# PSUM tiles of one bank in the attention and channel stages, made over into pairs for the last phase

## The chip, the cores and the metric

The kernel runs on one core of a Trainium2 chip. PE (TensorE) multiplies into PSUM, a memory of eight banks of 512 float32 columns on 128 partitions; DVE (VectorE) and ACT (ScalarE) read results out of it; POOL (GpSimd) works on data in SBUF; SP issues the DMAs. The metric is the time of one execution on the device, in microseconds (us), as a median over runs.

## What is computed

Attention under a mask of blocks, then a mixer over tokens and channels, then an RWKV layer. The weights of the mixer and of the last layer are 64-bit floating-point words; the kernel splits each into a high and a low float32 part on the chip, and what they multiply too, so that a product takes three matmuls.

```python
# B, H, S, D = 4, 8, 576, 64; a position sees the blocks of 64 up to its own
attn = softmax(mask(q @ k.T / 8)); x = (attn @ v) as [B, S, 512]
h = relu(x.T @ w_tok1) @ w_tok2              # tokens: 576 -> 256 -> 576
u = x + h.T
u = u + relu(u @ w_ch1) @ w_ch2              # channels: 512 -> 1536 -> 512
xp = u moved on by one token
k = relu((mu_k * u + (1 - mu_k) * xp) @ w_k) # 512 -> 1024
r = sigmoid((mu_r * u + (1 - mu_r) * xp) @ w_r)
out = r * (k * k @ w_v)
```

## The kernel before, in words

Attention works on 16 pairs of heads. For a pair, PE multiplies q by k into PSUM (`emit_s`), DVE takes each row's maximum while it applies the mask and writes the shifted scores to SBUF (`emit_max`, L376), ACT takes the exponential (L381), POOL scales by the reciprocal of the sum (L390), PE transposes the result into PSUM (`emit_t`, L399 and L401), ACT or DVE copies it to SBUF (tiles pt), and PE multiplies by v, both heads and several blocks accumulating in one bank (`emit_pv`), copied into the tile u of the batch. For every two pairs the token mixing of their columns comes in between the work on later pairs: PE transposes u (L655), ACT and DVE split the transposed data into a high and a low part (xnh, xnl, the latter by L673), PE multiplies (k1), ACT and DVE split again (h1h L700, h1l L704), PE multiplies (k2), and DVE adds the result to u (ku, L729).

The channel stage (L, O) goes over five slabs of 460 or 464 tokens: for each of twelve blocks of 128 hidden channels a product into a bank of the lower half, split by ACT (L966) and DVE (L969), then four products that accumulate over the blocks in four banks of the upper half; at a slab's end DVE adds these to u (L996). The last phase goes over the four batches with products K, V and R, seven block products each, whose results stand in two banks side by side and are read by one instruction over both (`wide`; L1122 and L1126, for instance). Weights come page by page: a DMA, some integer work on ACT, DVE and POOL, and a split by POOL or ACT and by L218.

The order of all work is set beforehand. The class `Plan` holds every operation with its cost, priority and buffers, and plays them on a clock of its own; an operation is recorded on its engine when the planned time of all that it needs has come. PSUM is the ring `one` of eight slots, each a bank. A slot is given out when all users of the one before are done in the planned time; among free ones the longest free is taken. `lo4` and `hi4` take of the lower and the upper half, `two` takes two adjacent slots. Slots 6 and 7 are held for the score blocks of full width, 576 columns, until attention's last maximum.

Planned times only fix the order on each engine. What an engine waits for when the kernel runs is put in afterwards by the framework, from the instructions' reads and writes of tiles. In the kernel before PSUM consists of four tiles of two banks (L274), and a slot is half of one:

```python
banks = [ps1.tile([128, 2, 512], F32, name=f"bank{k}") for k in range(4)]
def bank(key):
    i = plan.slot["one", key]
    return banks[i // 2][:, i % 2]
def wide(key):
    return banks[plan.slot["one", key] // 2][:, :, 0:T]
```

Of the kernel before, what the change touches and what calls it, by code (L numbers as in the profile page):

```python
# [8 lines left out]
F32 = mybir.dt.float32  # L9
# [8 lines left out]
PSUM = bass.MemoryType.PSUM  # L18
# [4 lines left out]
T = 288  # L23
# [43 lines left out]
class Plan:  # L67
# [40 lines left out]
    def slots(self, n, done):  # L108

        want, got, at = {}, [], 0.0  # L110
        for tag, _ in self.ops[n][4]:
            want[tag] = want.get(tag, 0) + 1
        for tag, k in want.items():
            can = []
            ring, part = self.PART.get(tag, (tag, None))
            for i in range(len(self.taken[ring])) if part is None else part:
                keys = {x for x in self.taken[ring][i:i + 1 + (tag == "two")] if x}
                users = [u for key in keys for u in self.users[key]]
                if all(u in done for u in users):
                    can.append((max([done[u] + self.LAT for u in users], default=0.0), i))  # L120
            if len(can) < k:
                return None, tag
            can.sort()
            got += [(tag, i) for _, i in can[:k]]
            at = max(at, can[k - 1][0])
        return at, got
# [10 lines left out]
    def run(self):  # L137
        ops = self.ops
        waiting = {n: len(set(o[1])) for n, o in ops.items()}
        after = {n: [] for n in ops}  # L140
        for n, o in ops.items():
            for d in set(o[1]):
                after[d].append(n)
        ready = {n for n, w in waiting.items() if not w}
        done, free, where, now = {}, {}, {}, "f"
        self.taken = {t: [None] * n for t, n in self.rings.items()}
        for tag, i, key in self.held:
            self.taken[tag][i] = key
        self.order = []
        while len(done) < len(ops):  # L150
            best, starts = None, {}
            for n in ready:
                room = 0.0
                if ops[n][4]:
                    room, _ = self.slots(n, done)
                    if room is None:
                        continue
                can = []
                for e, c in ops[n][0].items():
                    at = max(room, free.get("turn", 0.0) if self.turns(n, e) else 0.0)  # L160
                    r = max([at] + [done[d] + (0.0 if where[d] == e else ops[d][5]) for d in ops[n][1]])
                    pri = ops[n][3]
                    if e == "PE":
                        c += self.SWITCH * (self.mode[n] != now)
                        pri -= 0.25 * (self.mode[n] == now)
                    can.append((max(r, free.get(e, 0.0)), pri, n, c, e))
                end = min(x[0] + x[3] for x in can)
                for x in can:
                    if x[0] + x[3] <= end + 0.2:
                        starts.setdefault(x[4], []).append(x[:4])  # L170
            for e, cand in starts.items():
                first = min(c[0] for c in cand)
                t, p, n, c = min((c for c in cand if c[0] <= first + 0.02), key=lambda c: (c[1], c[0], str(c[2])))
                if best is None or (t, p, str(n), t + c, e) < best[:5]:
                    best = (t, p, str(n), t + c, e, n, c)
            if best is None:
                raise RuntimeError("stuck: " + "\n".join(f"{n} {self.slots(n, done)[1]}" for n in ready))
            t, _, _, _, e, n, c = best
            if ops[n][4]:
                got = self.slots(n, done)[1]  # L180
                for (tag, i), (_, key) in zip(sorted(got), sorted(ops[n][4], key=lambda a: a[0])):
                    ring = self.PART.get(tag, (tag,))[0]
                    self.taken[ring][i] = key
                    self.slot[ring, key] = i
                    if tag == "two":
                        self.taken[ring][i + 1] = key
            if e == "PE":
                now = self.mode[n]
            free[e] = t + c
            if self.turns(n, e):  # L190
                free["turn"] = t + c
            done[n], where[n] = t + c, e
            ready.remove(n)
            for m in after[n]:
                waiting[m] -= 1
                if not waiting[m]:
                    ready.add(m)
            self.order.append((t, e, n))
            self.record(ops[n][2], e)
# [3 lines left out]
def attn_mixer_rwkv_kernel(ctx: ExitStack, tc: tile.TileContext, z, v, vl, wt1, wt2, wc1, wc2, wk, wv, wr, mu, out):  # L203
    nc = tc.nc
    PE, ACT, DVE, POOL, SP = nc.tensor, nc.scalar, nc.vector, nc.gpsimd, nc.sync
    plan = Plan(tc)
# [13 lines left out]
    def mm(o, l, r, start, stop, more=False):  # L220
        PE.matmul(o, lhsT=l, rhs=r, start=start, stop=stop, skip_group_check=more)  # L221
# [48 lines left out]
    vs = [att2.tile([128, 4, 128], F32, name=f"vs{s}") for s in range(3)]  # L270
    vd = [att2.tile([128, 5, 128], F32, name=f"vd{s}") for s in range(3)]
    att3 = tc.alloc_tile_pool(name="att3", bufs=1, side="right")
    ps1 = tc.alloc_tile_pool(name="ps1", bufs=1, space=PSUM)
    banks = [ps1.tile([128, 2, 512], F32, name=f"bank{k}") for k in range(4)]  # L274
    pools = {}
    tl = {}


    def bank(key):

        i = plan.slot["one", key]
        return banks[i // 2][:, i % 2]

    def wide(key):

        return banks[plan.slot["one", key] // 2][:, :, 0:T]

    def warm(k):
        t = bank(("warm", 0))
# [48 lines left out]
    def s_part(p, h, i, cut):  # L338

        t, zt, hs = tl["s", p, h, i], tl["z", p], slice(64 * h, 64 * h + 64)  # L340
        q = zt[hs, S - 64 + 128 * i:S + 64 + 128 * i]
        k0 = (S - KE[i]) * h
        return [(t[:, COL[i] + a:COL[i] + e], q, zt[hs, k0 + a:k0 + e], True, True) for a, e in zip(cut, cut[1:])]

    def emit_s(p, step):
        if step < 2:
            a, b = (0, 1) if step == 0 else (1, 0)
            tl["s", p, a, 4] = banks[3].rearrange("p a b -> p (a b)")
            tl["s", p, b, 3] = tl["s", p, b, 0] = bank(("c", p, b, 3))
            x = s_part(p, a, 4, (0, 288, 576))  # L350
            y = s_part(p, b, 3, (0, 224, 448)) + s_part(p, b, 0, (0, 64))
        else:
            x, y = [], []
            for h, w in ((0, x), (1, y)):
                tl["s", p, h, 2] = tl["s", p, h, 1] = bank(("c", p, h, 2))
                w += s_part(p, h, 2, (0, 320)) + s_part(p, h, 1, (0, 192))
        for k in range(max(len(x), len(y))):
            for w in (x, y):
                if k < len(w):
                    mm(*w[k])  # L360
# [22 lines left out]
    def emit_rec(p, h, a, e):  # L383
        st = tl["st", p, h]
        DVE.tensor_tensor(st[:, 2, a:e], st[:, 1, a:e], eps[:, a:e], ALU.add)  # L385
        DVE.reciprocal(st[:, 2, a:e], st[:, 2, a:e])
# [55 lines left out]
    for p in range(NP):  # L442
        w = p - 3
# [9 lines left out]
        for h in range(2):  # L453
            for i in range(5):
                step = 2 if i in (1, 2) else (h if i == 4 else 1 - h)
                key = ("c", p, h, {0: 3, 1: 2}.get(i, i))
                f = p - 1.9 + 0.1 * step + 0.03 * {4: 0, 3: 1, 0: 2, 2: 0, 1: 1}[i] + 0.01 * h
# [5 lines left out]
                    lambda e, p=p, h=h, i=i: emit_max(p, h, i), f,  # L463
# [5 lines left out]
            for g, (a, b) in enumerate(((0, 3), (3, 5))):  # L469
                add(("rc", p, h, g), "DVE", 0.36, [("e", p, h, i) for i in range(a, b)],  # L470
                    lambda e, p=p, h=h, a=a, b=b: emit_rec(p, h, a, b), p - 2.5, uses=[("st", p, h)])
        for g, (diag, off) in enumerate(GROUPS):
# [3 lines left out]
                lambda e, p=p, g=g: emit_t(p, g), p - 1.0 + 0.07 * g,  # L476
# [163 lines left out]
    for b in range(B):  # L640
        for g in range(2):
# [33 lines left out]
            for c2 in range(3):  # L675
                n = 512 if c2 < 2 else 256
                key = ("xt", b, g, c2)
# [3 lines left out]
                    lambda e, f=xh, c2=c2: f(e, c2=c2), pb - 3, alloc=[] if c2 else [("xn", xk)], uses=[key] + ([xk] if c2 else []))  # L681
# [24 lines left out]
            for m in range(2):  # L706
                key, hk = ("k1", b, g, m), ("h1", b, g, m)
# [23 lines left out]
            for c in range(2):  # L731
                for p in range(2):
                    key = ("k2", b, g, p, c)
                    add(key, "PE", 6 * c_mm(T), [(s, b, g, m) for s in ("h1h", "h1l") for m in range(2)]
                        + [(s, "t2", 2 * c + k) for s in ("hi", "lo") for k in range(2)],
                        lambda e, f=k2, p=p, c=c: f(e, p=p, c=c), pb + 0.2 + 0.01 * c, alloc=[("dense", key)],
                        uses=[("h1", b, g, 0), ("h1", b, g, 1)], lat=0.3)
                    add(("ku", b, g, p, c), "DVE", c_dve(T), [key] + [("xt", b, g, k) for k in range(3)],
                        lambda e, f=ku, p=p, c=c: f(e, p=p, c=c), pb - 3, uses=[key])
# [21 lines left out]
    for nm, f in pages:  # L761
        tag = ("w" if f < 8 else "wx") if nm == "c1" else "w2a" if f < 4 else "w2b"
# [11 lines left out]
        n, k = PAIR.get((nm, f), (0, 0))  # L774
# [34 lines left out]
    for i in range(B):  # L809
        for n in range(7):  # L810
            for q in range(2):
                name = ("ld", "k", i, q, n)
                fetch_op(name, last + made_in("k", q, n, 0), ("W", "k", i, q, n), ("k", q, n, 0), "w", None if i == 0 else 130.0 + 16 * i - 9 + 0.1 * n)
                last = [name]
        for n in range(7):
            name = ("ld", "r", i, n)
# [116 lines left out]
    for t in range(NX):  # L933
        w = XS[t]
# [21 lines left out]
        for f in range(12):  # L956
            key, hk = ("lb", t, f), ("h", t, f)
# [26 lines left out]
        for f in range(12):  # L984
            for ms in ([(m,) for m in range(4)] if f in (0, 11) else [(0, 1, 2, 3)]):
# [3 lines left out]
                    lambda e, f=f, O=O, ms=ms: O(e, f=f, ms=ms), p0 + 1.2 + 0.5 * f + 0.01 * ms[0],  # L989
# [49 lines left out]
    for i in range(B):  # L1039
        b = order[i]  # L1040
# [233 lines left out]

    plan.run()
    pools["w2b"].release()
    ps1.release()
    pools["xp"].release()
    wp.release()
    glob.release()  # L1280
# [51 lines left out]
```

## Time and profile before

| what | us |
|---|---|
| median of 3 runs | 796.91 (794.59 to 796.92) |
| the profiled execution in all | 796.9 |
| its span, first to last instruction | 795.1 |
| PE busy | 761.4 |
| PE weight loads busy | 698.9 |
| DVE, ACT, POOL busy | 535.1, 399.5, 275.6 |

A stage's rate is set by the engine that is never idle in it; the idle time of the others costs nothing. So the table says little by itself, and the windows by stage and the list of waits say where PE stands and for whom. A matmul's end is modelled, and matmuls overlap: records of 0.28 us may follow each other every 0.12 us. In the rows, L221 is the helper that records most matmuls, so that the names of the tiles tell them apart: `bank<-z` are scores, `bank<-pt,vs` and `bank<-pt,vd` the products with v, `bank<-xnh,w1h` the first product of the token mixing, `bank<-w2h,h1h` the second, `bank<-xhl,w` and `bank<-hpB,w` those of the channel stage and the last phase. L211 and L213 are the helpers that copy on ACT and DVE.

### The profile page before, as it was taken

Reading aid. Unit: us, or ns where it says so; the run is one execution under the profiler, and the core shown is the slowest. Engines: PE = TensorE matmul, PEld = TensorE weight load, DVE = VectorE, ACT = ScalarE, POOL = GpSimd, SP = SyncE. Lnnn points to the kernel's source line nnn. Section 1 sums busy time; section 2 is a strip of 40 time slices with the busy share of each in tenths; the row PEclk is TensorE's granted clock in tenths of the full one; section 3 lists DMA queues with packets and bytes.
Section 4 is the critical chain, followed back from the end, with each engine's and each line's share of the span. In section 5 each row is a group of like instructions: output and inputs, shape, how many; then the busy total and the mean of one; then the engine's idle time right before and its main releaser. Section 6 shows DMA issues by size and latency. Waiting matters only on the chain.

```text
span 795.1 us, 14514 instructions
## 1 busy us (share of the span) xinstructions
PE 761.4 (96%) x5452; PEld 698.9 (88%) x5452; DVE 535.1 (67%) x1144; ACT 399.5 (50%) x863; POOL 275.6 (35%) x347
## 2 busy tenths in 40 slices
PE   9899798888998999999999999999999999999997
PEld 6778687877987888888888888888999999999997
DVE  4778677765736667955747666311498898898894
ACT  4667674566643345314223233111378576676772
POOL 4567464745636554624414321000020030120120
PEclk9999999999999999999999999999999999999999
DMA  6343341522101334253555453262784785755821
GB/s 191 87 128 96 100 128 52 157 92 87 54 28 54 107 133 153 86 200 146 217 199 172 161 196 146 85 211 102 241 289 138 256 283 186 258 174 204 299 75 46
DMA packets 53237, 119.56 MB, mean 150 GB/s; under 512 B 15408, under 2 KB 19504, under 8 KB 53168
## 3 DMA queue, kind: packets, MB, share of 16 engines
q1 hardware_dynamic: 53168, 118.64, 44.6%
q8 instruction: 43, 0.70, 0.4%
q14 instruction: 26, 0.21, 0.1%
HBM read 94.38 MB, written 24.25 MB: 149 GB/s over the span
## 4 chain that ended last, share of the span: by engine, by line
PE 90%; DVE 5%; ACT 3%; issue 1%; POOL 1%; DVEq 0%; ACTq 0%; POOLq 0%
PE bank L221 84%; PE bank L399 4%; DVE P L376 1%; DVE pt L213 1%; PE bank L401 1%; PE bank L655 1%; ACT pt L211 1%; POOL P L390 1%; ACT P L381 1%; DVE xnl L673 1%; ACT xnh L211 0%; ACT h1h L700 0%; DVE h1l L704 0%; DVE u L729 0%; DVE xnh L673 0%
## 5 line engine op out<-in xcount | busy, mean ns | idle before, releaser
L221 PE MATMUL bank<-xhl,w 128*128 128x288 f32 (+2 forms) x1776 | 280.6, 316 | 0.3 <-DVE hpB L969 0.3
L221 PEld LDWEIGHTS bank<-xhl,w 128*128 128x128 f32 x1776 | 263.7, 188 | 11.4 <-DVE hpB L969 0.7
L221 PE MATMUL bank<-hpB,w 128*128 128x460 f32 (+2 forms) x720 | 136.8, 341 | 0.0
L221 PEld LDWEIGHTS bank<-hpB,w 128*128 128x128 f32 x720 | 120.3, 188 | 9.8
L390 POOL TENSOR_SCALAR P<-P,st 128x448 f32<-128x448 f32 (+4 forms) x160 | 83.5, 540 | 75.3 <-DVE st L385 29.0
L376 DVE CUSTOM_DVE_ANT_0 P<-bank,mask 128x576 f32<-128x576 f32 (+4 forms) x160 | 72.3, 485 | 35.7 <-PE bank L221 24.4
L381 ACT ACTIVATE P<-P,st 128x576 f32<-128x576 f32 (+4 forms) x160 | 88.4, 557 | 14.1 <-DVE st L376 14.1
L522 POOL TENSOR_TENSOR td<-td,raw 128x512 int32<-128x512 int32 (+2 forms) x37 | 45.2, 1223 | 76.7 <-DVE td L518 48.8
L966 ACT ACTIVATE hpB<-bank 128x460 fp32r<-128x460 f32 (+1 forms) x36 | 20.0, 556 | 90.7 <-PE bank L221 87.7
L221 PE MATMUL bank<-hpA,w 128*128 128x460 f32 (+1 forms) x288 | 63.9, 372 | 0.0
L399 PE MATMUL bank<-ident,P 128*128 128x128 f32 x320 | 50.5, 280 | 14.0 <-DVE st L376 5.1
L221 PE MATMUL bank<-z 64*128 64x224 f32 (+4 forms) x448 | 59.7, 382 | 0.9 <-DVE u L213 0.4
L221 PEld LDWEIGHTS bank<-hpA,w 128*128 128x128 f32 x288 | 54.0, 188 | 6.2
L221 PEld LDWEIGHTS bank<-z 64*128 64x128 f32 x448 | 47.2, 189 | 12.2 <-issue 5.6
L969 DVE SCALAR_TENSOR_TENSOR hpB<-bank,hpB 128x460 fp32r<-128x460 f32 (+1 forms) x36 | 22.9, 636 | 51.4 <-ACT hpB L966 49.8
L211 ACT COPY pt<-bank 128x448 f32<-128x448 f32 (+1 forms) x61 | 33.0, 559 | 44.9 <-PE bank L221 16.8
L399 PEld LDWEIGHTS bank<-ident,P 128*128 128x128 f32 x320 | 35.2, 140 | 21.1 <-issue 7.8
L221 PE MATMUL bank<-xhl,wx 128*128 128x460 f32 (+1 forms) x240 | 53.3, 371 | 0.0
L969 DVE SCALAR_TENSOR_TENSOR hpA<-bank,hpA 128x460 fp32r<-128x460 f32 (+1 forms) x24 | 15.3, 637 | 53.8 <-ACT hpA L966 53.8
L221 PEld LDWEIGHTS bank<-xhl,wx 128*128 128x128 f32 x240 | 45.1, 188 | 5.2
L966 ACT ACTIVATE hpA<-bank 128x460 fp32r<-128x460 f32 (+1 forms) x24 | 13.3, 554 | 69.0 <-PE bank L221 64.9
L221 PE MATMUL bank<-pt,vs 128*64 128x128 f32 x640 | 45.2, 276 | 2.3 <-DVE st L376 1.0
(198 smaller groups left out, 1287.5 us busy)
## 6 DMA issues: line engine op xcount, KB each, us to landing
w<-pages SPq DMA_DIRECT2D x96, 512.0 KB, 4.7
pages<-raw SPq DMA_DIRECT2D x40, 256.0 KB, 2.4
z<-in_z SPq DMA_DIRECT2D x16, 576.0 KB, 3.9
raw<-in_wc SPq DMA_DIRECT2D x18, 512.0 KB, 3.7
pages<-rawx SPq DMA_DIRECT2D x30, 256.0 KB, 2.3
vs<-in_v SPq DMA_DIRECT2D x16, 256.0 KB, 3.3
out<-u SPq DMA_DIRECT2D x14, 288.0 KB, 2.4
rawx<-in_wc SPq DMA_DIRECT2D x6, 512.0 KB, 4.5
```

The source lines that it names most:

```text
L211: ACT.copy(o, i)
L213: DVE.tensor_copy(o, i)
L221: PE.matmul(o, lhsT=l, rhs=r, start=start, stop=stop, skip_group_check=more)
L376: DVE.tensor_tensor_reduce(p_view(p, h, i), s_view(p, h, i), m, -0.125, 3.0e38, ALU.add, ALU.min, tl["st", p, h][:, 0, i:i + 1])
L381: ACT.activation(w, w, ACTF.Exp, bias=st[:, 0, i:i + 1], scale=-1.0, accum_out=st[:, 1, i:i + 1])
L390: POOL.tensor_scalar(w, w, tl["st", p, h][:, 2, i:i + 1], 1.0, ALU.mult, ALU.mult)
L399: PE.transpose(t[:, o + 128 * k:o + 128 * k + 128], tl["P", p, i][:, c:c + 128], ident)
L401: PE.transpose(t[:, 64 * k:64 * k + 128], tl["P", p, i][:, 128 * i:128 * i + 128], ident)
L522: POOL.tensor_tensor(td.bitcast(I32), td.bitcast(I32), lw, ALU.add)
L655: PE.transpose(t[0:rows, 256 * k + 128 * p:256 * k + 128 * p + 128], u[b][:, 2 * g + p, c:c + rows], ident)
L966: ACT.activation(tl["h", t, f][0], tl["lb", t, f][:, 0:w], ACTF.Relu)
L969: DVE.scalar_tensor_tensor(tl["h", t, f][1], tl["lb", t, f][:, 0:w], 0.0, f32(tl["h", t, f][0]), ALU.max, ALU.subtract)
```

## The change

PSUM is now allocated as two pools. The left one has four tiles of one bank, slots 0 to 3; the right one has slots 4 and 5 as tiles of one bank, and slots 6 and 7 as one tile of two, for the wide score block. When the last phase first asks for two adjacent slots of a half, that half's pool is released and allocated again as two tiles of two banks. The plan knows of this: as long as a half has not been made over, a pair in it is free only when all four slots of the half are.

```diff
@@ in Plan.slots
                 keys = {x for x in self.taken[ring][i:i + 1 + (tag == "two")] if x}
+                if tag == "two" and i // 4 not in self.paired:
+                    keys = {x for x in self.taken[ring][i // 4 * 4:i // 4 * 4 + 4] if x}
                 users = [u for key in keys for u in self.users[key]]
@@ in Plan.run
+        self.paired = set()
...
                     if tag == "two":
                         self.taken[ring][i + 1] = key
+                        self.paired.add(i // 4)
@@ in attn_mixer_rwkv_kernel
-    ps1 = tc.alloc_tile_pool(name="ps1", bufs=1, space=PSUM)
-    banks = [ps1.tile([128, 2, 512], F32, name=f"bank{k}") for k in range(4)]
+    psums = [tc.alloc_tile_pool(name=f"ps{k}", bufs=1, space=PSUM, side=side) for k, side in enumerate(("left", "right"))]
+    banks = [psums[k >= 4].tile([128, 512], F32, name=f"bank{k}") for k in range(6)]
+    banks.append(psums[1].tile([128, 1024], F32, name="bank67"))
+    pairs = {}
...
     def bank(key):
         i = plan.slot["one", key]
-        return banks[i // 2][:, i % 2]
+        return banks[i] if i < 6 else banks[6][:, 512 * i - 3072:512 * i - 2560]
 
     def wide(key):
-        return banks[plan.slot["one", key] // 2][:, :, 0:T]
+        i = plan.slot["one", key] // 2
+        if i not in pairs:
+            z = i // 2
+            psums[z].release()
+            psums[z] = tc.alloc_tile_pool(name=f"ps{z}w", bufs=1, space=PSUM, side=("left", "right")[z])
+            for k in (2 * z, 2 * z + 1):
+                pairs[k] = psums[z].tile([128, 2, 512], F32, name=f"pair{k}")
+        return pairs[i][:, :, 0:T]
...
-            tl["s", p, a, 4] = banks[3].rearrange("p a b -> p (a b)")
+            tl["s", p, a, 4] = banks[6]
...
-    ps1.release()
+    psums[1].release()
+    psums[0].release()
```

No instruction changes its place: each engine has the same instructions in the same order as before, and up to the last phase each works in the same bank. The names of tiles and the semaphores that an instruction waits for (in brackets, by the engine or DMA queue that releases them) are other ones. In the rows below the number behind a tile's name is a running one; `bank1_122` is the tile of slots 2 and 3 before, `bank3_127` the tile of slot 3 after.

On PE, in the second half of the products with v of one pair of heads (at 142.95 us in the trace of before), there stands before:

```order
L221 MATMUL bank2_123<-z_1408 128x224
L221 MATMUL bank2_123<-z_1408 128x64
L221 MATMUL bank0_121<-pt51_108,vd0_112 64x64 [waits DVE_49]
L221 MATMUL bank0_121<-pt51_108,vd0_112 64x64
L221 MATMUL bank1_122<-pt51_108,vs0_109 64x128 [waits DVE_49]
L221 MATMUL bank1_122<-pt51_108,vs0_109 64x128
L221 MATMUL bank1_122<-pt51_108,vd0_112 64x64 x2
```

and now:

```order
L225 MATMUL bank5_129<-z_1414 128x224
L225 MATMUL bank5_129<-z_1414 128x64
L225 MATMUL bank0_124<-pt51_108,vd0_112 64x64 [waits Activation_49]
L225 MATMUL bank0_124<-pt51_108,vd0_112 64x64
L225 MATMUL bank3_127<-pt51_108,vs0_109 64x128 x2
L225 MATMUL bank3_127<-pt51_108,vd0_112 64x64 x2
```

The first of the products with vs waited for DVE before, and waits for nothing now (so that it stands in one row with the next). The product before it, into slot 0, waits for ACT in place of DVE.

On PE, at the end of the first product of a token mixing and at the transposition of u that follows (238.6 us in the trace of before), there stands before:

```order
L221 MATMUL bank3_124<-xnh_2543,w1l_81 128x256
L655 MATMUL bank2_123<-ident_62,u3_61 128x128 x4
L655 MATMUL bank2_123<-ident_62,u3_61 128x128 [waits Activation_49]
L655 MATMUL bank2_123<-ident_62,u3_61 128x128 x3
L655 MATMUL bank1_122<-ident_62,u3_61 64x128 [waits DVE_49]
L655 MATMUL bank1_122<-ident_62,u3_61 64x128
```

and now:

```order
L225 MATMUL bank67_130<-xnh_2549,w1l_81 128x256
L668 MATMUL bank4_128<-ident_62,u3_61 128x128 [waits DVE_49]
L668 MATMUL bank4_128<-ident_62,u3_61 128x128 x3
L668 MATMUL bank5_129<-ident_62,u3_61 128x128 [waits DVE_49]
L668 MATMUL bank5_129<-ident_62,u3_61 128x128 x3
L668 MATMUL bank2_126<-ident_62,u3_61 64x128 [waits DVE_49]
L668 MATMUL bank2_126<-ident_62,u3_61 64x128
```

The first four transpositions go into slot 4, the next four into slot 5. The latter waited for ACT, which reads slot 4; now they wait for DVE, as the former do.

On PE, at the end of the channel stage and in the first products K of the last phase (564 us in the trace of before), there stands before:

```order
L221 MATMUL bank2_123<-hpB_2688,w_3408 128x464 x6
L221 MATMUL bank0_121<-xhl_2685,w_4730 128x288 [waits DMAHW0_49]
L221 MATMUL bank0_121<-xhl_2685,w_4730 128x288 x11
L221 MATMUL bank1_122<-xhl_2685,w_4746 128x288 [waits DMAHW1_49]
L221 MATMUL bank1_122<-xhl_2685,w_4746 128x288 x11
L221 MATMUL bank3_124<-xhl_2685,w_4762 128x288 [waits DMAHW2_49,DVE_49]
L221 MATMUL bank3_124<-xhl_2685,w_4762 128x288 x11
L221 MATMUL bank2_123<-xhl_2685,w_4778 128x288 [waits DMAHW3_49,DVE_49]
```

and now:

```order
L225 MATMUL bank4_128<-hpB_2694,w_3414 128x464 x3
L225 MATMUL bank5_129<-hpB_2694,w_3414 128x464 x3
L225 MATMUL pair0_5071<-xhl_2691,w_4736 128x288 [waits DMAHW0_49,PE_49]
L225 MATMUL pair0_5071<-xhl_2691,w_4736 128x288 x11
L225 MATMUL pair1_5072<-xhl_2691,w_4752 128x288 [waits DMAHW1_49]
L225 MATMUL pair1_5072<-xhl_2691,w_4752 128x288 x11
L225 MATMUL pair2_5107<-xhl_2691,w_4768 128x288 [waits DMAHW2_49,DVE_49]
L225 MATMUL pair2_5107<-xhl_2691,w_4768 128x288 x11
L225 MATMUL pair3_5108<-xhl_2691,w_4784 128x288 [waits DMAHW3_49]
```

The first product has gained a wait for PE's own earlier instructions. The third pair of slots is now 4 and 5, where it was 6 and 7, and the fourth has lost its wait for DVE, which the third one's covers.

In all, 692 rows of PE's order have a wait, where 623 had one, and 170 of them wait for two semaphores or more, where 146 did.

## Rows read from the trace of the kernel before

**Rows 1.** The page's first part: busy us of each engine.
```profile
PE 761.4 (96%) x5452; PEld 698.9 (88%) x5452; DVE 535.1 (67%) x1144; ACT 399.5 (50%) x863; POOL 275.6 (35%) x347
```

**Rows 2.** Windows by stage: us, busy us (instructions) of five engines, clock, DMA.
```profile
0.00:260.00 260.00, 231.42 (x2306) 201.59 (x2307) 172.32 (x619) 155.38 (x454) 147.41 (x245) 0.99 0.32 96
240.00:260.00 20.00, 15.79 (x118) 14.80 (x119) 13.68 (x26) 7.58 (x16) 12.88 (x11) 1.00 0.16 53
260.00:560.00 300.00, 299.69 (x1442) 268.78 (x1441) 169.96 (x266) 91.79 (x160) 92.82 (x82) 1.00 0.45 156
560.00:795.20 235.20, 230.24 (x1708) 228.52 (x1706) 192.83 (x259) 152.33 (x249) 35.33 (x20) 1.00 0.60 203
```

**Rows 3.** Chain of waits, 255 to 320 us: start us, us, what.
```profile
259.56 60.49 PE bank L221 x299
```

**Rows 4.** Waits of PE, 0 to 260 us: total us, times, longest.
```profile
PE bank L399 <- DVE st L376: 5.1, 5, 1.5
PE bank L399 <- POOL P L390: 3.7, 4, 1.0
...
PE bank L221 <- DVE wz L298: 1.4, 1, 1.4
...
PE bank L399 <- ACT xnh L211: 0.3, 1, 0.3
```

**Rows 5.** Timeline, 143.5 to 144 us: start, us, instruction [idle <-releaser].
```profile
143.50 0.35 DVE L376 CUSTOM_DVE_ANT_0 P<-bank,mask 128x192 f32<-128x192 f32 x1
...
143.78 0.08 DVE L376 DVE_READ_ACCUMULATOR2_ANT st<- 128x1 f32 x1
...
143.92 0.44 PE L221 MATMUL bank<-pt,vs 128*64 128x128 f32 x4 [0.64 <-DVE st L376]
```

**Rows 6.** Timeline, 238.7 to 241 us.
```profile
238.75 0.60 PE L655 MATMUL bank<-ident,u 128*128 128x128 f32 x4
...
240.11 0.58 ACT L211 CAST xnh<-bank 128x512 fp32r<-128x512 f32 x1
...
240.74 0.88 PE L655 MATMUL bank<-ident,u 128*128 128x128 f32 x6 [1.39 <-ACT xnh L211]
```

**Rows 7.** Timeline: three stalls of PE, apart from each other.
```profile
22.07 0.95 PE L399 MATMUL bank<-ident,P 128*128 128x128 f32 x4 [0.74 <-POOL P L390]
...
85.71 0.34 PE L221 MATMUL bank<-pt,vd 128*64 128x64 f32 x4 [0.78 <-DVE xnl L673]
...
247.53 0.39 PE L221 MATMUL bank<-xnh,w1h 128*128 128x256 f32 x1 [0.55 <-DVE u L729]
```

**Rows 8.** Source line L399 on PE: ns shortest/median/longest, first and last start.
```profile
L399 PE MATMUL bank<-ident,P x320: 270/273/413, 16.0 to 228.7; 128*128 128x128 f32 x160
```

**Rows 9.** Chain of waits, 206 to 207.1 us.
```profile
206.59 0.11 PE bank L401
206.70 0.33 PE bank L399 x3
```

**Rows 10.** Timeline, 167.4 to 168.8 us.
```profile
167.44 0.42 DVE L673 TENSOR_TENSOR xnh<-bank,xnh 64x256 fp32r<-64x256 f32 x1
...
168.00 0.84 PE L399 MATMUL bank<-ident,P 128*128 128x128 f32 x6 [1.56 <-DVE xnh L673]
```

**Rows 11.** Timeline, 564 to 572 us, DVE and PE.
```profile
564.57 2.46 DVE L996 TENSOR_TENSOR u<-bank,u 128x464 f32<-128x464 f32 x4 [10.16 <-PE bank L221]
...
565.63 6.56 PE L221 MATMUL bank<-xhl,w 128*128 128x288 f32 x48
```

**Rows 12.** Timeline, 314 to 321 us, DVE and PE.
```profile
314.25 1.79 DVE L218 TENSOR_TENSOR w<-td,w 128x512 fp32r<-128x512 f32 x1
...
316.12 5.19 PE L221 MATMUL bank<-hpB,w 128*128 128x460 f32 x24
```

**Rows 13.** Windows around the fall of the clock, columns as in rows 2.
```profile
20.00:23.90 3.90, 2.32 (x21) 1.69 (x18) 3.43 (x19) 3.54 (x13) 2.41 (x6) 1.00 0.53 152
23.90:27.40 3.50, 3.50 (x19) 2.87 (x20) 1.89 (x10) 3.13 (x12) 3.09 (x6) 0.51 0.02 8
```

## The prediction

> **What bounds the kernel now.** I read the page first: TensorE (PE) is busy for 761.4 us, 96% of the span of 795.1 us, more than any other engine by 226 us [rows 1]. The windows by stage then say where the other 33.7 us are. Up to 260 us, through attention and the token mixing, PE is busy for 231.42 of 260 us; from 260 to 560 us, the channel stage, for 299.69 of 300; in the last phase for 230.24 of 235.2, and these 5 us are the output after the last matmul [rows 2]. The chain of waits agrees: from 259.56 us on it is one unbroken piece of PE [rows 3]. So the end of the kernel is where PE is done, and a microsecond taken out of PE's path before 260 us comes off the end, if the channel stage's weights are there that much earlier.
>
> The waits of PE name what holds it up to 260 us: 22 lines, 39 waits, 28.0 us in all, of which these are the first and the last lines, POOL's and the start's [rows 4]. Of the 28.58 us that PE is idle there, 28.0 is therefore a wait with a name, and all but 3.7 (POOL) and 1.4 (the start) is a wait for DVE or ACT. What is odd is whom it waits for. At 143.92 a PV matmul in the middle of an accumulation stands for 0.64 us until DVE has read a score maximum, a datum with which it has nothing to do; it starts 0.06 us after that read's end at 143.86 [rows 5]. At 240.74 a transposition of u stands for 1.39 us until ACT has copied the four transpositions before it, finished 1.4 us earlier [rows 6]. In both places reader and writer use different banks (slots 2 and 3, slots 4 and 5), but these two banks are one tile, and in the order the matmul's wait is for the reader of the neighbour.
>
> **The change part by part.** *Moves.* None: on every engine the instructions stand in the order they had. Attention, token mixing and channel stage keep their slots as well, and in the last phase the third and fourth pairs change places. What changes is who waits for whom.
>
> *Waits that go.* With one tile a bank the PV matmul waits for nothing and the transposition of u for an older reader of its own bank, as the order shows. I held each of the 39 stalls against its place in the two orders and the slots. Those that stay: the start (1.4 us); a transposition that waits for its own input from POOL (0.74 us at 22.07); two that wait for DVE's read of their own bank (0.78 us at 85.71, the other short, put at 0.2); and one on the tile of banks 6 and 7, which stays double (0.55 us at 247.53) [rows 4, 7]. Together 3.7. The other three waits of POOL's line are doubled ones, in which the bank's wait came last. This leaves 34 stalls and, of the 28.58 us, 24.9.
>
> *What a stall hides.* A matmul's record runs on after the next could have been issued: a transposition's lasts 0.27 us [rows 8], but back to back they follow each other every 0.11 us (three in 0.33) [rows 9]. The idle time before a late matmul is counted from the end of that record, so each stall costs some 0.16 us more than it shows: 34 x 0.16 = 5.4 us. Sum so far 30.3 us. Bounds: nothing hidden, 24.9; every stall on the longest record, 0.41 less 0.11, 35.
>
> *What is late next.* A PE that arrives earlier meets true inputs. Four stalls on true inputs or banks stand in the trace after the start (0.74, 0.78, 0.2, 0.55, mean 0.57). I let as many again appear, 2.3 us lost. Nothing lost is one bound. The other is half of the 34 stalls with such a wait behind them, 17 x 0.57 = 10 us. I take the small value since DVE, the busiest of the others, works for 172.32 of 260 us and would for 172 of 232, 74% [rows 2]: nobody else is the pace.
>
> *Added waits.* Where a wait for a whole tile stood for all its readers, the order now has one for each bank: 692 rows of PE wait instead of 623, 170 instead of 146 of them for two semaphores or more. A satisfied one costs nothing that shows: a transposition with a wait for POOL takes 0.11 us in a run like its neighbours without [rows 9]. A doubled one that does hold PE lets it go later, 0.14 us after the release at 167.86 against 0.06 for a single one [rows 5, 10]. I take nothing; the bound is 24 x 0.08 = 1.9 us. Behind a waiting matmul stand all later ones of PE, so each of these would count in full.
>
> *The making over.* The first two pairs need the four left banks to be done with; in the order their first matmul has gained one wait, for PE's own earlier work, which is done in turn anyway. The third pair is used after 24 of the 48 matmuls that begin at 565.63 and take 6.56, so at about 568.8, and now needs all four right banks: DVE's last addition out of them ends at 567.03 [rows 11]. 1.8 us are to spare, and all of it moves forward together. Cost nothing; had it no cover, at most the 2.46 us of these additions. That it frees nothing for DVE and ACT in the last phase is sure: the tiles there are as wide as before.
>
> *Sum.* 24.9 + 5.4 - 2.3 = 28.0 us. The profiled execution took 796.9 us in all, 1.8 of it around the span, and is as long as the median of the runs shown (796.91; 794.59 to 796.92). 796.9 - 28.0 = 768.9.
>
> A rule sets the size otherwise. PE's weight loads are busy for 201.59 of 260 us in the first stage, 77.5%, and for 268.78 of 300, 89.6%, in the stage where PE never waits [rows 2]. The Trainium skill (Perfetto Trace Analysis, Identifying the Most-Contended Engine) says that matmul busy time is a poor measure of headroom, since matmuls are pipelined, and that the busy share of the weight loads is a good one. By it, if the first stage came up to 89.6%, it would take 225 us instead of 260: 35 us less, where the idle time alone gives 25. My sum lies between them.
>
> **The rivals.** *Denser still.* The first stage reaches the weight-load share of the second: 201.59/0.896 = 225 us, 35 us off, 762 us. For it: nothing but PE's stalls separates the stages. Against it: attention's small matmuls need not load as densely, and the start stays.
>
> *The weights come no earlier.* A page of the second channel weight is finished at 316.04, and PE starts on it at 316.12 [rows 12]. These pages are loaded only once attention's last outputs are out. What PE gains before that point moves the loads too; what it gains after may be lost at the pages. From 240 to 260 us PE idles for 20 - 15.79 = 4.2 us [rows 2]; less the 0.55 that stays and with 0.16 unseen for each of four stalls that is 4.3. 796.9 - (28.0 - 4.3) = 773.2. Against it: the engines that make the pages lose waits of the same kind.
>
> *Inputs take over.* The 10 us bound of above, and the doubled waits: 30.3 - 10 - 1.9 = 18.4, so 778.5. For it: POOL does 3.7 us of waits already; against it DVE's 66%.
>
> *The clock.* From 23.9 to 27.4 us PE was granted 0.51, the 1.2 GHz level, after a stretch in which it was busy for 2.32 of 3.90 us [rows 13]; this is the only such fall before the tail and costs 3.5 x 0.49 = 1.7 us. If PE, ahead of its inputs, gathered its short stalls into a few long ones, the clock would fall for each. It takes 17 falls (28.0/1.7), one for each of the 16 head pairs and one more, to make the kernel slower; at 20 it would be 803. Against it: the change only takes waits away, and no stall of up to 1.56 us elsewhere brought a fall. The Trainium skill (TensorE: Matmul & The Clock Gate, A second HAM failure mode: psum-queue depth-cycling) tells of a kernel whose clock swung because PE paused briefly between groups while it went round the PSUM banks. That speaks for fewer stalls and so for the change; here 39 of them brought one fall.
>
> *Nothing.* The waits that go had all another one just behind: 797.
>
> **How the numbers follow.** Forecast 768.9 (0.72; its own range 764 to 772), denser 0.09, weights 0.09, inputs 0.06, clock 0.02, nothing 0.02. The range that leaves out at most 2 in 10 reaches from the dense case to just past the one of the weights: 762 to 775. About 0.3%, 2.4 us, is what a measurement of this kernel can tell from no change. Faster 0.96, same 0.02, slower 0.02.
>
> **What would show it.** Right: in the profile after, PE idle for some 4 to 7 us in what takes the place of the first 260 us, the chain turning into one piece of PE near 232 us, no wait of a PV matmul for DVE's maxima and none of a transposition of u for ACT's copy of the group before; the stretches behind as long as now. Wrong: as many PE waits as before with other names (inputs), PE waits on the channel weights at 285 to 320 us (weights), a granted clock of 0.5 more than once (clock), or a PE wait at the first pairs of the last phase.

## The result and the profile after

The changed kernel takes 758.94 us (median of four runs, 758.15 to 759.29), the kernel before, beside it, 795.75 (794.21 to 796.92): a ratio of 0.9537, 95% interval 0.9514 to 0.956. The forecast was 768.9 with a range of 762 to 775. The direction and the place were right; the gain is 10 us larger than the forecast's sum, and 3 us beyond the low end, the "denser" case.

The profiled executions took 796.9 and 759.16 us, with spans of 795.1 and 757.1: 38.0 us between them. The page's line of busy times, which answers to [rows 1]:

```profile
PE 748.8 (99%) x5452; PEld 695.7 (92%) x5452; DVE 532.1 (70%) x1144; ACT 398.9 (53%) x863; POOL 277.7 (37%) x347
```

Busy and idle time of PE both fell. Busy went from 761.4 to 748.8, 12.6 us, though the same 5452 matmuls are done; idle (span less busy) from 33.7 to 8.3, 25.4 us. The windows by stage, as in [rows 2], with the first stage now ending near 222 us:

```profile
0.00:222.00 222.00, 218.57 (x2302) 197.87 (x2303) 171.44 (x619) 154.52 (x454) 146.42 (x243) 1.00 0.37 112
222.00:260.00 38.00, 38.00 (x196) 34.56 (x195) 24.62 (x42) 14.42 (x27) 21.68 (x21) 1.00 0.38 126
260.00:522.00 262.00, 262.00 (x1252) 234.81 (x1252) 143.36 (x227) 77.54 (x135) 74.27 (x64) 1.00 0.46 160
522.00:757.10 235.10, 230.19 (x1708) 228.49 (x1706) 192.66 (x259) 152.39 (x249) 35.31 (x20) 1.00 0.60 204
```

All but some 0.6 us of the gain is in the first stage. The channel stage is PE without a gap (before 0.31 us of idle in 300), and the last phase has 230.19 us of PE where it had 230.24, so the making over costs nothing that shows. In the first stage PE idles for 222 - 218.57 = 3.4 us. Its waits there, all of them, against the 22 lines of [rows 4] (columns: total us, times, longest):

```profile
PE bank L225 <- DVE wz L311: 1.4, 1, 1.4
PE bank L668 <- DVE xnl L686: 0.6, 1, 0.6
PE bank L225 <- DVE u L742: 0.6, 1, 0.6
PE bank L414 <- POOL P L403: 0.5, 2, 0.3
PE bank L412 <- DVE pt L217: 0.4, 1, 0.4
```

No PV matmul (a product with v) waits for a maximum (st) and no transposition of u (L668) for ACT's copy. The chain of waits (start us, us, what) has one last piece that is not PE, DVE's read of u, the wait on the tile that stayed double; from 212.80 us on it is PE alone, where before it was from 259.56 [rows 3]:

```profile
212.29 0.47 DVE u L742
...
212.80 2.54 PE bank L225 x19
215.34 1.09 PE bank L668 x10
216.43 43.78 PE bank L225 x239
```

One thing has to be known of the kernel before to read these 38.0 us: its executions lie in two groups, near 794.5 and near 797 us, and the profiled one, from which my sums started, is of the second.

### The profile page after: what moved, and what is told of

Read it like the earlier page. It is cut to its first block, busy times and chain, and to the rows that moved or that the text cites. A ratio compares the mean times of both kernels' runs of the same rounds, so it can differ in the third digit from the quotient of the medians.

```text
span 757.1 us, 14545 instructions
## 1 busy us (share of the span) xinstructions
PE 748.8 (99%) x5452; PEld 695.7 (92%) x5452; DVE 532.1 (70%) x1144; ACT 398.9 (53%) x863; POOL 277.7 (37%) x347
## 4 chain that ended last, share of the span: by engine, by line
PE 98%; DVE 1%; POOL 1%; ACT 0%; issue 0%; DVEq 0%; POOLq 0%
PE bank L225 61%; PE pair L225 30%; PE bank L412 5%; PE bank L668 1%; PE bank L414 1%; POOL P L403 1%; ACT pt L215 0%; ACT P L394 0%; DVE u L1266 0%; DVE u L1261 0%; DVE xnl L686 0%; DVE xnh L217 0%; DVE pt L217 0%; DVE wz L311 0%; DVE u L742 0%
## 5 line engine op out<-in xcount | busy, mean ns | idle before, releaser
L225 PE MATMUL pair<-xhl,w 128*128 128x288 f32 x1296 | 176.5, 295 | 0.0
L225 PEld LDWEIGHTS pair<-xhl,w 128*128 128x128 f32 x1296 | 173.7, 188 | 0.6
L225 PE MATMUL bank<-xhl,w 128*128 128x460 f32 (+1 forms) x480 | 104.1, 371 | 0.0
L225 PEld LDWEIGHTS bank<-xhl,w 128*128 128x128 f32 x480 | 90.0, 188 | 10.2
L394 ACT ACTIVATE P<-P,st 128x576 f32<-128x576 f32 (+4 forms) x160 | 88.4, 557 | 13.9 <-DVE st L389 13.5
L225 PE MATMUL bank<-hpB,w 128*128 128x460 f32 (+1 forms) x432 | 95.4, 372 | 0.0
L225 PEld LDWEIGHTS bank<-hpB,w 128*128 128x128 f32 x432 | 81.1, 188 | 9.6
L389 DVE CUSTOM_DVE_ANT_0 P<-bank,mask 128x576 f32<-128x576 f32 (+4 forms) x160 | 70.5, 483 | 15.8 <-PE bank L225 13.7
L225 PE MATMUL bank<-z 64*128 64x224 f32 (+4 forms) x448 | 55.3, 376 | 0.0
L225 PEld LDWEIGHTS bank<-z 64*128 64x128 f32 x448 | 44.6, 186 | 9.0 <-issue 3.8
```

What stands on the lines that cost most here:

```text
L389: DVE.tensor_tensor_reduce(p_view(p, h, i), s_view(p, h, i), m, -0.125, 3.0e38, ALU.add, ALU.min, tl["st", p, h][:, 0, i:i + 1])
L394: ACT.activation(w, w, ACTF.Exp, bias=st[:, 0, i:i + 1], scale=-1.0, accum_out=st[:, 1, i:i + 1])
```

## The experiments

### The double tiles back, all or some

`all_double`, `left_double`, `pair01_double` and `pair45_double` are the changed kernel with three, two or one of the left and middle tiles as tiles of two banks again; the planner's rule and the making over stay.

```diff
-    banks = [psums[k >= 4].tile([128, 512], F32, name=f"bank{k}") for k in range(6)]
+    twos = {z: psums[z >= 2].tile([128, 2, 512], F32, name=f"two{z}") for z in (0, 1, 2)}   # or (0, 1), (0,), (2,)
+    banks = [None if k // 2 in twos else psums[k >= 4].tile([128, 512], F32, name=f"bank{k}") for k in range(6)]
...
+        if i // 2 in twos:
+            return twos[i // 2][:, i % 2]
```

> The changed kernel with slots 0/1, 2/3 and 4/5 again as tiles of two banks; the making over before the last phase, its rule for slots and the third and fourth pairs changed about stay. Theory (false waits for the neighbour bank are all): as long as before, 796 us within 2.4, PE idle in the first 260 us again near 28 us, the fall of the clock at 24 us back. Rival (something in the making over pays or costs): off by more than 2.4 us, and the last phase other than 230.2 us of PE.

Measured: 794.60 us, ratio to the kernel before 0.9993 (0.9978 to 1.0008). The time of before is back with the tiles, so the making over neither pays nor costs anything that shows. The one thing expected that did not come is the fall of the clock: the profiled execution has none, and is 2.3 us shorter than the profiled one of before. The same window of both (kernel before first; columns as in [rows 2], the granted clock third from the end):

```profile
23.50:27.50 4.00, 3.71 (x21) 3.11 (x23) 2.39 (x12) 3.53 (x14) 3.49 (x7) 0.57 0.05 17
```

```profile
23.50:27.50 4.00, 4.00 (x51) 3.49 (x48) 3.14 (x11) 2.84 (x11) 3.09 (x5) 1.00 0.00 1
```

PE did 51 matmuls here instead of 21. Its page has the same idle time as before, 792.8 - 759.1 = 33.7 us, and 2.3 us less of busy time:

```profile
PE 759.1 (96%) x5452; PEld 697.3 (88%) x5452; DVE 535.0 (67%) x1144; ACT 399.5 (50%) x863; POOL 275.6 (35%) x347
```

So the fall costs 2.3 us, where [rows 13] gave 1.7, and without it the change is worth 794.6 - 758.9 = 35.7 us.

> The changed kernel with slots 4/5 alone as one tile of two banks. In the trace before, 7 of the stalls that fell away were on this tile, 4.55 us of idle. Theory A (a stall costs its idle and 0.16 us, as forecast): 4.55 + 7 x 0.16 = 5.7, so 764.6 us. Theory B (each microsecond of idle costs 37.7/25.2 = 1.5 us, whatever the cause): 6.8, so 765.8. Theory C (the rest of the gain is the clock's fall at 24 us): 764 without a fall, 1.7 more with one. If PE meets fewer or more stalls than before, the same sums with the idle and the count that the profile shows.

> The changed kernel with slots 0/1 alone as one tile of two banks: in the trace before 16 of the stalls that fell away, 10.9 us of idle. Theory A: 10.9 + 16 x 0.16 = 13.5, so 772.4 us. Theory B (1.5 us for each of idle): 16.4, so 775.3. By the idle and the count that the profile shows, should they differ.

> The changed kernel with slots 0/1 and 2/3 as two tiles of two banks and 4/5 as single banks: 31 of the stalls, 20.25 us of idle. Theory A: 20.25 + 31 x 0.16 = 25.2, so 784.1 us. Theory B: 30.4, so 789.3. A rival to both (the tiles' stalls stand in for each other, one tile's hides the other's): this and the kernel with 4/5 double together cost more than all three double.

Measured: 768.85, 769.37 and 779.28 us, so +9.9, +10.4 and +20.3 over the changed kernel (of the 20.3 about 1 is the fall of the clock: the two executions without it, at a granted clock of 1.000, took 778.24 and 778.32). The pages of 4/5 and of 0/1 alone (spans both 767.5 us, PE idle 13.9 and 16.4):

```profile
PE 753.6 (98%) x5452; PEld 696.7 (91%) x5452; DVE 530.9 (69%) x1144; ACT 398.1 (52%) x863; POOL 276.7 (36%) x347
```

```profile
PE 751.1 (98%) x5452; PEld 695.7 (91%) x5452; DVE 530.8 (69%) x1144; ACT 398.5 (52%) x863; POOL 275.9 (36%) x347
```

All three expectations fell. With 4/5 alone PE idles 13.9 - 8.3 = 5.6 us more and is busy 4.8 us longer, 1.8 us of time for each of idle; with 0/1 alone it is 8.1 and 2.3, 1.3 for each. There is no fixed factor (theory B), and the stalls of one tile, counted out of the trace of before, don't give its price (theory A said 5.7 and 13.5). Nor do the tiles add up: 20.3 + 9.9 = 30.2, and all three cost 35.7.

### Which wait it is

These kernels keep the tiles of one bank and put the double tile's waits back by hand, one kind at a time or several together. Each instruction gets them when it is recorded: `put` and `got` are the slots 0 to 5 that it writes and reads, `wrote` and `read` hold each slot's last matmul and last readers, and `k ^ 1` is the neighbour slot.

```diff
...
+        if pe:                                    # pe_waits, both_waits, three_waits
+            for k in put:
+                for n in self.read.get(k ^ 1, {}).values():
+                    self.tc.add_manual_dep(i, n, sync, reason="reader of the neighbour")
+        if not pe:                                # reader_waits, both_waits, three_waits
+            for k in got:
+                if k ^ 1 in self.wrote:
+                    self.tc.add_manual_dep(i, self.wrote[k ^ 1], sync, reason="writer of the neighbour")
+        if not pe:                                # between_readers, three_waits
+            for k in got:
+                for e, n in self.read.get(k ^ 1, {}).items():
+                    if e != str(i.engine):
+                        self.tc.add_manual_dep(i, n, sync, reason="reader of the neighbour")
...
```

> The changed kernel, tiles of one bank, but each matmul that writes one of the slots 0 to 5 is made to wait for the last DVE and ACT readers of the neighbour slot, as a tile of two banks made it. DVE and ACT stay free of their share of the false waits. Theory (PE's waits alone are the cost): as long as before, 794.6 us (the kernel with all three double tiles) within 2.4, PE idle near 28 us in the first 260 us. Rival (the tile also delays the readers, and so what PE waits for): below 792, the difference being the readers' part.

> The reverse: each DVE or ACT instruction that reads one of the slots 0 to 5 waits for the last matmul into the neighbour slot; PE's own waits stay as in the changed kernel. Theory (PE's waits alone): 758.9 us within 2.4. Rival (freed readers are why so little was late next: 1 or 2 us where I let 2.3 appear and bounded it by 10): 761 to 769, with PE waits for inputs in the profile.

> Tiles of one bank with both kinds of false wait put back by hand: matmuls wait for the neighbour slot's readers, and the readers for the neighbour slot's matmuls. Alone the first cost 10.9 us and the second 8.4. Theory (the two feed each other: a reader held back by the neighbour's matmuls is what the next matmul then waits for): 794.6 us within 2.4, as with three double tiles, so some 17 us more than the two alone. Rival (they add up, and the double tile costs something else besides): 758.9 + 10.9 + 8.4 = 778.

> The third kind alone: DVE and ACT wait for each other's last read of the neighbour slot, PE's waits and the readers' waits for PE as in the changed kernel. Theory (each kind costs little alone and much behind the others): 759 to 761. If it cost alone what it adds to the other two (794.6 less 790.3): 763.2.

> Tiles of one bank with three kinds of false wait by hand: matmuls for the neighbour slot's readers, readers for its matmuls, and now DVE and ACT each for the other's last read of the neighbour slot, which a tile of two banks also brought. Theory: with all three the kernel is again as long as with the double tiles, 794.6 us within 2.4 (the first two gave 790.3). Rival: it stays near 790, and the double tile has a cost that is no wait.

| kernel | us | over 758.9 | PE busy | PE idle |
|---|---|---|---|---|
| pe_waits | 769.82 | 10.9 | 753.2 | 14.8 |
| reader_waits | 767.36 | 8.4 | 754.6 | 12.1 |
| between_readers | 759.83 | 0.9 | 749.0 | 8.9 |
| both_waits | 790.27 | 31.3 | 759.8 | 30.9 |
| three_waits | 794.49 | 35.6 | 759.0 | 33.8 |

(The last two columns are of the profiled execution; those of reader_waits and both_waits had the fall of the clock, 0.57 and 0.61 in the window above.) Part of reader_waits' 8.4 is that fall: its two executions without one, at a granted clock of 0.999, took 765.75 and 766.18 us, 7.0 over. The 0.9 of between_readers is less than can be told from nothing between kernels that weren't run side by side. My theory that PE's waits are the cost fell: alone they bring back 10.9 of 35.7 us. So did the idea that the kinds add up: 10.9 + 8.4 + 0.9 = 20.2, together 35.6. The theory for both_waits fell too, as 790.27 is 4.3 short of 794.6; the third kind makes up the rest. With all three the time is that of the double tiles to 0.1 us, and PE's list up to 262 us has 39 waits again, where PE's kind alone gives 16 and the readers' alone 12. No other cost of the double tile shows.

How they feed each other is seen at the PV stall of [rows 5]. Timelines of PE and DVE at the same place of the program (start us, us, instruction, idle before and releaser). DVE's instruction with `P<-bank,mask` is the maximum. First the kernel before:

```profile
142.95 0.34 PE L221 MATMUL bank<-pt,vd 128*64 128x64 f32 x4
...
143.09 0.49 DVE L376 CUSTOM_DVE_ANT_0 P<-bank,mask 128x320 f32<-128x320 f32 x1 [0.18 <-PE bank L221]
```

DVE's maximum over one slot has been held up for 0.18 us until PE wrote into the neighbour; it and the next maximum are done at 143.86, and only then does PE's PV matmul go, 0.64 us late. With PE's waits alone:

```profile
127.69 0.48 DVE L407 CUSTOM_DVE_ANT_0 P<-bank,mask 128x320 f32<-128x320 f32 x1
...
128.38 0.34 PE L243 MATMUL bank<-pt,vd 128*64 128x64 f32 x4
128.55 0.39 PE L243 MATMUL bank<-pt,vs 128*64 128x128 f32 x4
```

The maximum ran 0.69 us before that PV piece instead of 0.14 behind it, and PE's false wait was met in time: no idle. With the readers' waits alone:

```profile
132.10 0.34 PE L243 MATMUL bank<-pt,vd 128*64 128x64 f32 x4
132.27 0.39 PE L243 MATMUL bank<-pt,vs 128*64 128x128 f32 x4
...
132.24 0.49 DVE L407 CUSTOM_DVE_ANT_0 P<-bank,mask 128x320 f32<-128x320 f32 x1 [0.26 <-PE bank L243]
```

Now DVE is held up by 0.26 us and PE goes on, since nothing makes it wait for that read. In the changed kernel neither waits:

```profile
123.44 0.48 DVE L389 CUSTOM_DVE_ANT_0 P<-bank,mask 128x320 f32<-128x320 f32 x1
...
124.11 0.34 PE L225 MATMUL bank<-pt,vd 128*64 128x64 f32 x4
124.28 0.39 PE L225 MATMUL bank<-pt,vs 128*64 128x128 f32 x4
```

At this place the two halves of a tile were worked in lockstep: the reader waits for the writer of the other half, and the writer then for that reader.

### What a stall costs beside its idle time

> Leaves the whole computation out and measures one wait by itself. Ten stretches of 24 groups of 6 transpositions 128x128 behind one another; the first of each group writes a bank that DVE has read in the group before, with reads of 0 (no wait), 64, 128, 192, 256, 320, 384, 448, 512 and 2 x 512 columns, so that the wait grows from nothing. Theory A (a stall costs its idle and 0.16 us): a group's time over the one without waits, less the idle that the trace shows, is 0.16 us in every stretch with idle, and 0 in those without. Theory B (cost is 1.5 times the idle): the excess grows with the idle. Theory C (waits that end while the matmul before still counts as busy cost time and show no idle, and a matmul after a stall starts slower): an excess of 0.2 to 0.3 us with idle, and up to 0.2 us in a stretch that shows none.

This one missed its aim: with no order given, free matmuls were moved into the waits, 7 behind one that waits instead of 5, until none were left. Only its single gaps could be used. With the order kept:

> The wait by itself again, with PE's order kept as written (in the first one matmuls had been moved into the waits): 13 stretches of 24 groups of 8 transpositions, DVE reads of 0, 128, 192, 256, 288, 320, 352, 384, 448, 512, 2 x 256, 2 x 320 and 2 x 384 columns. Leaves the whole computation out. The first one showed a late matmul 0.160 us behind its predecessor instead of 0.109, the next 0.165 behind it instead of 0.109, and no idle. Theory C: a group's time over the one without waits less the idle shown is 0 where nothing is late, rises to 0.11 to 0.22 while no idle shows, and stays at about 0.22 (0.16 under the record, 0.06 at the start after it) once idle shows. Theory A: 0.16 at most. Theory B: it grows on with the idle.

`keep` records an instruction and ties it to the one before it on its engine; `t` is the bank that DVE reads (tile read), `other` one that it doesn't.

```python
...
for _ in range(ROUNDS):
    keep(PE.transpose, t[:, 0:128], P, ident)
    for j in range(1, GROUP):
        keep(PE.transpose, other[:, 128 * (j % 4):128 * (j % 4) + 128], P, ident)
    for n in cols:
        keep(DVE.tensor_copy, got[:, 0:n], t[:, 0:n])
```

Timelines of PE: no wait at all (the first stretch), a read of 448 columns, two of 384. A group's time is the distance of two "read" rows:

```profile
16.59 0.27 PE L42 MATMUL read<-ident,P 128*128 128x128 f32 x1
16.70 0.93 PE L42 MATMUL other<-ident,P 128*128 128x128 f32 x7
17.47 0.27 PE L42 MATMUL read<-ident,P 128*128 128x128 f32 x1
...
190.06 0.33 PE L42 MATMUL read<-ident,P 128*128 128x128 f32 x1
190.22 0.93 PE L42 MATMUL other<-ident,P 128*128 128x128 f32 x7
191.10 0.33 PE L42 MATMUL read<-ident,P 128*128 128x128 f32 x1
...
308.74 0.33 PE L42 MATMUL read<-ident,P 128*128 128x128 f32 x1 [0.48 <-DVE got L42]
308.90 0.93 PE L42 MATMUL other<-ident,P 128*128 128x128 f32 x7
310.31 0.33 PE L42 MATMUL read<-ident,P 128*128 128x128 f32 x1 [0.48 <-DVE got L42]
```

Without a wait a group takes 0.873 us; so it does with reads of 128 to 256 columns, whose waits are met in time. With 448 it takes 1.045: 0.17 us dearer, and not a trace of idle. With 2 x 384 it takes 1.571 and shows 0.478 of idle: 0.220 more than it shows. Over the stretches (18 groups each, time over 0.873 less the idle):

| columns read | 288 | 320 | 352 | 384 | 448 | 512 | 2x256 | 2x320 | 2x384 |
|---|---|---|---|---|---|---|---|---|---|
| group us | 0.880 | 0.913 | 0.946 | 0.979 | 1.046 | 1.113 | 1.305 | 1.438 | 1.571 |
| idle shown | 0 | 0 | 0 | 0 | 0 | 0.020 | 0.212 | 0.345 | 0.478 |
| cost unseen | 0.006 | 0.039 | 0.073 | 0.106 | 0.172 | 0.220 | 0.220 | 0.220 | 0.220 |

Theory C held: once idle shows, 0.164 us lie under the record of the matmul before, and 0.056 come after, since the late matmul's record is 0.33 us long instead of 0.27 and the next starts 0.165 behind it instead of 0.109. Here a stall that costs less than 0.22 us in all shows no idle.

How much of this stands in the kernel itself can be read from two traces without a fall of the clock, those of `all_double` and of the changed kernel, by the distance of each matmul's start to the one before it. Over all 5452 matmuls these distances shrink by 35.8 us. At the matmuls before which either kernel's list has a wait, and at the one right behind each, they shrink by 30.0 us: 24.7 of listed idle and 5.3 that the idle doesn't show (6.0 if three behind are counted). At all others together they shrink by 5.7 us: 0.7 of it is idle of less than 0.15 us apiece, which the list of waits leaves out, and 5.0 shows no idle at all. One such place is a row of eight transpositions, first in `all_double`, then in the changed kernel:

```profile
53.16 1.31 PE L415 MATMUL two<-ident,P 128*128 128x128 f32 x8
...
53.81 0.42 PEld L415 LDWEIGHTS two<-ident,P 128*128 128x128 f32 x4 [0.24 <-DVE st L392]
```

```profile
47.87 1.09 PE L412 MATMUL bank<-ident,P 128*128 128x128 f32 x8
```

The row is 0.22 us longer and has no idle inside. The fifth transposition's weight load (PEld) had to wait for DVE; the matmul starts 0.272 us behind the fourth instead of 0.109, and the sixth 0.164 behind it instead of 0.109.

### The tile that stayed double

```diff
...
-        return banks[i] if i < 6 else banks[6][:, 512 * i - 3072:512 * i - 2560]
+        if i >= 6 and len(banks) == 7:
+            top[0].release()
+            top[0] = tc.alloc_tile_pool(name="ps2s", bufs=1, space=PSUM, side="right")
+            banks[6:] = [top[0].tile([128, 512], F32, name=f"bank{k}") for k in (6, 7)]
+        return banks[i]
...
```

> The changed kernel with banks 6 and 7, too, made over into two tiles of one bank as soon as attention's last scores that need both are done with. The one wait that stands on this tile in the profile (0.6 us, a matmul for DVE's read of the neighbour) goes, with 0.22 us that a stall costs beside its idle: 758.9 - 0.8 = 758.1. Rival (what comes next is late by as much, or the readers freed give more): 758.9, or 757.

Measured: 758.00 us (756.79 to 758.17, five runs; ratio to before 0.9529, 0.9516 to 0.9542), and the wait for u is gone from the list. The 0.9 us to 758.94 are about as expected, but the ranges of the two kernels touch, and they weren't run side by side: a better version probably, not certainly.

## Why the prediction was wrong in size

From the profiled execution of before, 38.0 us went: 25.4 of idle, 2.3 of the clock's fall and 10.3 more of busy time. The forecast had 28.0. Term by term:

- **What a stall hides, 5.4.** This step failed most. I took 0.16 us, the record's tail from [rows 8, 9], for each stall that shows idle, and had no term for a matmul that is late and shows none. For the stalls that I counted the size was right: 5.3 to 6.0 us in the kernel's own traces. What was missing are the 5.0 us (4.3 by the wider count) at matmuls before which no idle shows. Term: 10.3 in place of 5.4. (The 0.22 us of the wait by itself is not a price for all stalls: in the kernel the hidden part of one lies between 0.03 and 0.27.)
- **Waits that go, 24.9.** Near in size, and in part by luck. Of the five that I let stay, three stayed: the start, the short one and the tile of banks 6 and 7. The two others, 0.74 and 0.78 us, which I had read as waits for a true input and for PE's own bank, went as well, and with 0.3 us of the channel stage 26.7 us of idle went in all.
- **What is late next, -2.3.** In its place 1.2 us came up: two waits for P of 0.26 us, six and two matmuls behind waits that went (the first of these the one of 0.74), 0.37 us that is left of a wait of 1.48, and the short one 0.3 us longer. The reason given failed more than the size: I asked whether DVE was busy enough to become the pace, and held the readers' times fixed. But the change frees the readers as well, and inputs come sooner too. Put the readers' waits back alone and the kernel loses 7.0 to 8.4 us.
- **The clock, not in the sum.** Its 1.7 us [rows 13] were in my base and I let them stay. The fall comes in some executions of the old program and not in others; 2.3 us of the difference are that.
- **Added waits, the making over: 0.** Nothing shows: three double tiles with the making over take as long as the kernel before.

Together 4.9 + 1.8 + 1.1 + 2.3 = 10.1: the 10.0 us missing, but for rounding.

Of the rivals, "denser" came nearest. It used no stall at all, only the weight loads' share: from 77.5% to the channel stage's 89.6% [rows 2], 35 us. After, they are busy for 197.87 of 222 us, 89.1%, and without the clock the gain is 35.7. So in this one case the rule of the Trainium skill (Perfetto Trace Analysis, Identifying the Most-Contended Engine), that the busy share of the weight loads and not that of the matmuls measures the headroom, told the size better than my sum over stalls, which left out those without idle; I gave it 0.09 because attention's small matmuls need not load as densely, and after the change they nearly did. "Weights" fell (PE never waits in the channel stage), "inputs" too, and a clock below 1.00 stands in no window of the first three stages.

The mechanism I named, PE waiting for the neighbour's readers, brings back under a third of it by itself. That the idle of PE's listed waits came out close all the same is because those waits were the end of a loop, and the change takes the whole loop away. Its other half, readers that wait for the neighbour's matmuls, stood in DVE's rows, and I had looked at PE's alone. DVE's maxima wait for PE's products, true waits and false ones together, before and after (0 to 265 us; total us, times, longest):

```profile
DVE P L376 <- PE bank L221: 24.4, 22, 6.3
```

```profile
DVE P L389 <- PE bank L225: 13.7, 12, 6.2
```

## What to carry to other kernels

Where the parts of one buffer are written and read in turn, a wait for the whole buffer ties both sides: price the loop, not one side's waits, since either side alone gave back under a third of the 35.7 us. A stall of PE cost more here than its idle time, and a short one showed none (up to 0.22 us by itself); so a sum over listed waits fell 5 us short, and it is worth holding such a sum against an estimate from the densest stage of the same kernel. A base taken from one profiled execution carries what that execution alone had, here 2.3 us of a fall of the clock.

## What was not expected of the hardware

In the wait measured by itself, a transposition that is released late has a record of 0.33 us instead of 0.27, and its successor starts 0.056 us later than otherwise, for every stall that costs from 0.07 to 0.7 us.

The fall of the clock at 24 us comes and goes in one and the same program. Four profiled executions have it (before, left_double, reader_waits, both_waits); those of all_double and three_waits, which have the false waits too, don't. How busy PE was just ahead does not tell it: from 20 to 23.5 us that was 1.92 of 3.5 us in all_double, without a fall, and 2.21 in the kernel before, with one:

```profile
20.00:23.50 3.50, 2.21 (x20) 1.55 (x16) 3.03 (x17) 3.14 (x10) 2.01 (x5) 1.00 0.55 158
```

```profile
20.00:23.50 3.50, 1.92 (x16) 1.29 (x13) 3.38 (x21) 3.14 (x12) 2.42 (x6) 1.00 0.53 171
```

What decides it stays open.
